# Turning the slots of tokens in SBUF by VectorE, in place, instead of into PSUM by TensorE

## The chip, the cores and the metric

The kernel runs on one core of one Trainium2 chip. The metric is device time in microseconds, here the median of three executions: 631.35 us before the change (630.63 to 631.54).

## The reference

Two layers follow each other. The first is attention with a window of 64 positions (batch 8, 8 heads, 576 positions, head size 64). The second sends each of the 4608 tokens (512 wide) to the one of 8 experts that its gate prefers:

```python
logits = x @ w_gate + modality_bias[modality_id]
e_idx = np.argmax(logits, axis=1)
...
for e in range(E):
    mask = e_idx == e
    h = np.maximum(x[mask] @ w1[e], 0.0)
    out[mask] = gate_w[mask, None] * (h @ w2[e])
```

An expert has w1 of 512 x 1024 and w2 of 1024 x 512. All data are float32.

## The kernel before

**Attention.** The 4608 positions are 72 blocks of 64, and a step handles two of them (a pair, 128 tokens); there are 36 pairs and some steps of run-out. A step s does, in this order on TensorE: the product with the values of pair s-2 (`values`), the gate's logits of pair s-3, the scores of pair s (`scores`), the transposes of the probabilities of pair s-1, the transposes of the finished rows xa of pair s-2 (`x_t`), and two transposes of coming q or k heads (`heads_t`, copied out to qT or kT in `heads_out`). VectorE finds minima, copies qT and kT, divides (`values_out`, which writes xa) and does the routing. GpSimd scatters the finished rows, each with its gate and its token number behind it (514 floats), to `xs_scratch` in HBM, sorted by expert.

**Slots.** A slot is 256 rows of one expert that lie next to each other in `xs_scratch`. `slot_pieces` is a generator that writes the work of slots piece by piece; 16 pieces make a slot. From step 12 on, attention takes one piece at each of four gaps in a step (`gap`), so that a slot spans four steps; when attention is over, the pieces follow each other without attention between them. Two weight buffers hold the weights of two experts. In this execution 8 slots are read while attention runs, and 11 after it, the last of them with 128 rows. TensorE takes float32 data in one pass as fp32r; each product is therefore made of three, with every operand split into a high part (hi, rounded to fp32r) and the rest (lo). Per slot:

- `fetch` and `load_slot` (L250, L203) issue the load of the next slot's rows to xt from SP, ahead of need. xt has one buffer.
- The rows are turned, so that the model dimension lies on partitions. Partition p of piece c holds column 4p + c, to match the rows of w1; so a turn reads every fourth column, 16 bytes from element to element.
- `split` (L194) writes the high part xh (ScalarE, L195) and the low part xl (VectorE, L196) of the turned tokens.
- `first` (L306): 12 matmuls of 256 columns into one PSUM tile, called for k = 0 to 3 and i = 0, 1. After i = 1 comes relu to hh (ScalarE, L326) and the rest hl (VectorE, L327).
- `second` (L330): 6 matmuls of 512 columns from hh and hl into y, for both halves t of the slot, one k later.
- `finish` (L346): y times the gate on VectorE, and an indirect DMA from GpSimd to the output rows.

**Two ways to turn.** A slot that is fetched during attention is loaded by one DMA of 256 rows and turned by TensorE (L281): eight 128x128 transposes against the identity, four into a PSUM bank for each half of the model dimension. A slot that is fetched after attention is loaded by "quarters" (L210): four DMAs that each fill 32 partitions, token w*32 + p going to partition p of a quarter, with 128 columns (512 bytes) in each quarter, and a fifth DMA for gate and number. In this layout the turn needs 32x32 blocks only, and VectorE makes it (L276): four transposes of 128x256 from SBUF into two PSUM banks. Both ways end in PSUM, and the split reads PSUM.

**What sets the order.** The kernel writes the order of the instructions on all engines by hand (`manual_schedule`); each engine runs its own list in order. Work that must not stand in front of a piece's matmuls is put off: functions go to the list `later`, and `run_later` writes them out at fixed places in a step, behind the pieces. Within a slot with k = 3 the pieces are first(3,0), first(3,1), second(2,0), second(2,1), second(3,0), then first(0,0) and first(0,1) of the next slot, and second(3,1). The split's first half is put behind second(2,0), its second half behind second(2,1). The next slot is fetched before first(2,1) during attention and before first(1,0) afterwards. SP issues the loads of v, q, k, weights and slots on one queue, in the order in which the steps write them. The list `last` is empty until the steps of attention are written and non-empty from then on.

Of the kernel before, what the change touches and what calls it, by code (L numbers as in the profile page):

```python
# [8 lines left out]
F32 = mybir.dt.float32  # L9
F32R = mybir.dt.float32r  # L10
BF16 = mybir.dt.bfloat16
I32 = mybir.dt.int32
# [7 lines left out]
P = 128  # L20
# [6 lines left out]
def tile_window_attn_moe(  # L27
# [12 lines left out]
    nc = tc.nc  # L40
    B, H, S, D = q.shape
    N = B * S
    DM = H * D
# [3 lines left out]
    R32 = 32  # L47
    NR = P // R32
# [7 lines left out]
    TP = 2 * P  # L56
# [18 lines left out]
    NC1 = DM // P  # L75
# [53 lines left out]
    def tick(n=1, table=False):  # L129
        for _ in range(n):  # L130
            if routing and not table:
                routing.pop(0)()
            elif queue:
                queue.pop(0)()
                issued[0] += 1
# [58 lines left out]
    def split(ps, hi, lo):  # L194
        nc.scalar.copy(out=hi, in_=ps)  # L195
        nc.vector.tensor_tensor(out=lo, in0=ps, in1=hi.bitcast(F32), op=ALU.subtract)  # L196
# [6 lines left out]
    def load_slot(row_ap, late, nb, quarters):  # L203
        rb = nc.values_load(row_ap, engines=[ET.SP], min_val=0, max_val=DUMMY)
        xt = epool.tile([P, 2, ROW], F32, name="xt")
        rows = xs_blk[bass.ds(rb, nb)]
        if not quarters:
            parts = [(xt[:, 0:nb], rows.rearrange("b p c -> p b c"))]
        else:
            parts = [(x_of(xt)[r * R32:(r + 1) * R32, 0:nb].rearrange("p b w d c -> p b w (d c)"),  # L210
                      rows[:, :, r * P:(r + 1) * P].rearrange("b (w p) c -> p b w c", p=R32)) for r in range(NR)]
            parts.append((tail_of(xt)[:, 0:nb], rows[:, :, DM:ROW].rearrange("b p c -> p b c")))
        for dst, src in parts:
            ins = nc.sync.dma_start(out=dst, in_=src)
            if late is not None:
                tc.declare_no_dep(ins.ins, group=late, reason="rows written before are read")
                tc.add_to_no_dep_group("early_loads", ins.ins)
        return xt

    def x_of(xt):  # L220

        flat = xt.rearrange("p b c -> p (b c)")
        return flat[:, 0:2 * DM].rearrange("p (b w d c) -> p b w d c", b=2, d=R32, c=NC1)
# [5 lines left out]
    last = []  # L229
    position = [-4]  # L230
# [4 lines left out]
    later = []  # L235
    scattered = []

    def bank(i):

        if i == 0 or not last and i == 1:  # L240
            return ps_m.tile([P, 512], F32, name="em")
        if i == 1:
            return ps_s.tile([P, 512], F32, name="sp0")
        return ps_t.tile([P, 512], F32, name="tp")
# [5 lines left out]
    def fetch():  # L250
        if fetched:
            return fetched.pop(0)
        row, late, buf, whichever, need = todo.pop(0)
        assert late is not None or not pads
        assert late is None or late in scattered
        tick(need - issued[0], table=True)
        nb = 1 if whichever == NANY else 2
        quarters = bool(last)
        xt = load_slot(row, late, nb, quarters)
        return dict(xt=xt, buf=buf, any=whichever, nb=nb, quarters=quarters,  # L260
                    tail=tail_of(xt) if quarters else xt[:, :, DM:])

    def slot_pieces():


        def x_turn(sl, i, tp=None):

            xt, nb = sl["xt"], sl["nb"]
            if ("tp", i) in sl or nb == 1 and i == 0:
                return  # L270
            tp = sl["tp", i] = tp or bank(2 if i and (last or not sl["quarters"]) else 0)
            cs_ = range(2 * i, 2 * i + 2) if nb == 2 else range(NC1)
            for n, c in enumerate(cs_):
                cols = slice(n * nb * P, (n + 1) * nb * P)
                if sl["quarters"]:
                    nc.vector.transpose(  # L276
                        out=tp[:, cols].rearrange("p (w t) -> p w t", t=R32),
                        in_=x_of(xt)[:, 0:nb, :, :, c].rearrange("p b w d -> p (b w) d"))
                    continue
                for t in range(nb):  # L280
                    nc.tensor.transpose(  # L281
                        out=tp[:, cols][:, t * P:(t + 1) * P].bitcast(F32R),
                        in_=xt[:, t, c:DM:NC1].bitcast(F32R), identity=ident_r)

        def x_split(sl, i):

            nb = sl["nb"]
            x_turn(sl, i)
            if i == 0:
                sl["x"] = [epool.tile([P, NC1 * TP], F32R, name=nm) for nm in ("xh", "xl")]  # L290
                if nb == 1:
                    return
            hi, lo = (x[:, (2 * i * TP if nb == 2 else 0):][:, 0:512] for x in sl["x"])
            split(sl.pop(("tp", i)), hi, lo)
            if i == 1:
                sl["gate"] = epool.tile([P, 2], F32, name="gate", bufs=2)
                nc.gpsimd.tensor_copy(out=sl["gate"][:, 0:nb], in_=sl["tail"][:, 0:nb, 0])
                sl["id"] = epool.tile([P, 2], I32, name="id", bufs=2)
                nc.gpsimd.tensor_copy(out=sl["id"][:, 0:nb], in_=sl["tail"][:, 0:nb, 1])

        def x_part(sl, i, tp=None):
            if not sl["quarters"]:
                x_turn(sl, i, tp)
            later.append(lambda: x_split(sl, i))

        def first(sl, k, i):  # L306

# [104 lines left out]
        NK = NC2 // 2  # L412

        sl = fetch()
# [8 lines left out]
        while True:  # L423
            nxt = None
            for k in range(1, NK):
                for i in range(2):
                    if (k, i) == ((1, 0) if last else (2, 1)) or k == 2 and i == 1 and nxt is None:
                        assert todo
                        nxt = fetch()
                    first(sl, k, i)  # L430
                    if k == NK - 1 and i == 0 and last and nxt["quarters"]:
                        later.append(lambda: (x_turn(nxt, 0), x_turn(nxt, 1)))
                    yield
                for t in range(2):
                    second(sl, k - 1, t)
                    if k == NK - 1 and nxt and t == 1:
                        x_part(nxt, 1)
                    yield
                    if k == NK - 1 and nxt and t == 0:
                        x_part(nxt, 0)  # L440
                        run_later()
            second(sl, NK - 1, 0)
            yield
            if nxt["nb"] == 1:
                break
            first(nxt, 0, 0)
            yield
            first(nxt, 0, 1)
            yield
            second(sl, NK - 1, 1)  # L450
            yield
            sl = nxt
# [31 lines left out]
    epool = actx.enter_context(tc.tile_pool(name="epool", bufs=1))  # L484
# [402 lines left out]
    def keep_warm(n):  # L887
# [5 lines left out]
    ident_r = const.tile([P, P], F32R, name="ident_r")  # L893
# [5 lines left out]
        out=brow, in_=mod_bias.rearrange("(o m) e -> o m e", o=1).broadcast_to([P, 2, E]))  # L899
# [19 lines left out]
    for h in range(2):  # L919
# [3 lines left out]
        for m in range(3):  # L923
            nc.gpsimd.affine_select(
                out=masks[rows, m, own], in_=masks[rows, m, own],
# [4 lines left out]
            else:  # L930
                nc.gpsimd.affine_select(
                    out=masks[rows, m, before], in_=masks[rows, m, before],
# [5 lines left out]
    for t in xas:  # L938
# [4 lines left out]
        out=tri, in_=tri, compare_op=ALU.is_gt, fill=0.0, base=0,  # L943
# [79 lines left out]
    for s in range(NPR + 4):  # L1023
# [52 lines left out]
        if heads:  # L1076
            tp = turn_bank(s)
# [8 lines left out]
        if R >= 0:  # L1086
            tp = turn_bank(s)
# [10 lines left out]
        if heads:  # L1098
            tp = turn_bank(s)
# [138 lines left out]
    while next(it, "end") != "end":  # L1238
        run_later()
        tick(4)  # L1240
        t = position[0]
# [3 lines left out]
        for n in range(RAWS):  # L1245
            if n < len(swaps) and n == len(ahead) and swaps[n][0] <= t + RAWS:
                _, buf, x, c = swaps[n]
# [18 lines left out]
    with tc.If(trip > 0):  # L1266
        NS = N // P + E
        with ExitStack() as gctx:
# [4 lines left out]
            for st in (1, 2, 4):  # L1273
# [4 lines left out]
            cs_ = gen.tile([1, E], F32, name="cs_")  # L1278
# [22 lines left out]
                out=eoff, in0=desc[0:1, 0, :], scalar1=-1.0, scalar2=float(E), op0=ALU.mult, op1=ALU.add)  # L1301
# [3 lines left out]
                out=gtab[:, :, 1], in0=rw, scalar1=float(E - 1), scalar2=None, op0=ALU.min)  # L1305

            with tc.For_i(0, trip, 1) as it:
# [3 lines left out]
                xt = gen.tile([P, ROW], F32, name="gxt")  # L1311
# [7 lines left out]
                for c in range(NC1):  # L1319
                    wt = gen.tile([P, F], F32, name="gw1", bufs=2)  # L1320
                    nc.sync.dma_start(out=wt, in_=w1_v[bass.ds(ee, 1), :, c, :].rearrange("o p f -> (o p) f"))
                    for n in range(F // 512):
                        nc.tensor.matmul(
                            out=hps[n], lhsT=xT[:, c * P:(c + 1) * P], rhs=wt[:, n * 512:(n + 1) * 512],
# [5 lines left out]
                for n in range(F // 512):  # L1330
                    tp = gps.tile([P, 512], F32, name="gxp")
# [5 lines left out]
                for c2 in range(NC2 // 2):  # L1337
                    wt = gen.tile([P, 2, DM], F32, name="gw2", bufs=2)
                    nc.sync.dma_start(
                        out=wt, in_=w2_v[bass.ds(ee, 1), :, 2 * c2:2 * c2 + 2, :].rearrange("o p c f -> (o p) c f"))  # L1340
                    for i in range(2):
                        c = 2 * c2 + i
                        nc.tensor.matmul(
                            out=yp, lhsT=hT[:, c * P:(c + 1) * P], rhs=wt[:, i, :],
# [3 lines left out]
                    out=y, in0=yp, scalar1=xt[:, DM:DM + 1], scalar2=None, op0=ALU.mult)  # L1348
# [3 lines left out]
                    out=out, out_offset=bass.IndirectOffsetOnAxis(ap=oi, axis=0),  # L1352
                    in_=y, in_offset=None, bounds_check=N - 1, oob_is_err=False)
# [31 lines left out]
```

## Time and profile before

| what | value |
|---|---|
| median of 3 runs | 631.35 us (630.63 to 631.54) |
| the profiled execution's own time | 630.53 us |
| its span, first to last instruction | 628.8 us |
| TensorE (PE) busy | 611.0 us, 97%, 6429 matmuls |
| VectorE (DVE) busy | 383.9 us, 61% |
| ScalarE (ACT) busy | 296.8 us, 47% |
| GpSimd (POOL) busy | 136.1 us, 22% |
| SP's DMA queue | 67.45 MB, 41.6% of the DMA engines' time |

Rows of a timeline read: start in us, length in us, engine, line, operation, out<-in by tile names, shape, count; in brackets the idle time of the engine just before, and what ended it. PE is matmuls and transposes on TensorE, and matmuls are pipelined, so that rows overlap. Names of tiles: xt is a slot's rows, xh and xl the split tokens, hh and hl the split hidden layer, em, tp, sp and y PSUM tiles, xa finished attention rows, Whi and Wlo the split weights.

### The profile page before, as it was taken

The numbers are of one execution on the slowest core, as the hardware profiler recorded it, in microseconds if no ns is written. First come the engines' busy times: TensorE is split into PE (matmuls) and PEld (weight loads), VectorE is DVE, ScalarE is ACT, GpSimd is POOL, SyncE is SP. The second block draws the span as 40 slices with busy tenths as digits, with TensorE's granted clock in tenths as the row PEclk, the third lists the DMA queues.
The fourth block names the chain that finished last, engine by engine and source line by source line (L and its number), as shares of the span: only waits on it lengthen the run. The fifth ranks groups of instructions, "written<-read, shape, count | busy, mean of one in ns | idle before, by whom it ended". The sixth has DMA issues, their size and how long they took to land. (4 is left out here: it accounts for less than half of the span.)

```text
span 628.8 us, 17271 instructions
## 1 busy us (share of the span) xinstructions
PE 611.0 (97%) x6429; PEld 549.2 (87%) x6429; DVE 383.9 (61%) x1493; ACT 296.8 (47%) x933; POOL 136.1 (22%) x315
## 2 busy tenths in 40 slices
PE   8899799999999999999999999999999999999996
PEld 5788688989898899989898899999899999989986
DVE  4899878766676765656655266324434743876721
ACT  4899785656556554645553111111113522564411
POOL 5423412222222320320323130011011011101102
PEclk9999999999999999999999999999999999999999
DMA  9999846675467544452412132732332653578300
GB/s 177 220 240 242 236 123 181 173 200 171 111 163 194 143 120 103 136 152 60 127 53 85 51 102 71 217 118 67 85 118 76 191 165 96 190 244 252 112 11 27
DMA packets 150230, 88.07 MB, mean 140 GB/s; under 512 B 120010, under 2 KB 130816, under 8 KB 150016
## 3 DMA queue, kind: packets, MB, share of 16 engines
q1 hardware_dynamic: 141568, 67.45, 41.6%
q0 software_dynamic: 5888, 18.93, 8.0%
q8 instruction: 51, 0.84, 0.5%
q10 hardware_dynamic: 2688, 0.58, 0.5%
q14 instruction: 35, 0.29, 0.2%
HBM read 67.49 MB, written 23.91 MB: 145 GB/s over the span
## 5 line engine op out<-in xcount | busy, mean ns | idle before, releaser
L340 PE MATMUL y<-Whi,hh 128*128 128x512 f32 x288 | 117.0, 406 | 0.0
L649 ACT ACTIVATE ss<-ss,mn 128x128 f32<-128x128 f32 x288 | 112.6, 398 | 2.0 <-DVE mn L637 2.0
L340 PE MATMUL y<-Wlo,hh 128*128 128x512 f32 x288 | 112.7, 391 | 0.0
L340 PE MATMUL y<-Whi,hl 128*128 128x512 f32 x288 | 112.6, 391 | 0.0
L351 POOL DMA_INDIRECT out_dram<-y,id x36 | 37.4, 1040 | 248.3 <-DVE y L348 165.4
L327 DVE SCALAR_TENSOR_TENSOR hl<-em,hh 128x512 fp32r<-128x512 f32 x50 | 34.5, 690 | 92.3 <-ACT hh L326 89.6
L318 PE MATMUL em<-xh,Whi 128*128 128x256 f32 x400 | 83.7, 291 | 0.0
L326 ACT ACTIVATE hh<-em 128x512 fp32r<-128x512 f32 x50 | 29.6, 593 | 106.1 <-PE em L318 102.1
L318 PE MATMUL em<-xl,Whi 128*128 128x256 f32 x400 | 79.3, 279 | 0.0
L318 PE MATMUL em<-xh,Wlo 128*128 128x256 f32 x400 | 79.2, 279 | 0.0
L637 DVE CUSTOM_DVE_ANT_0 ss<-sp,masks 128x128 f32<-128x128 f32 x288 | 63.6, 286 | 11.9 <-PE sp L623 10.5
L658 ACT COPY pT<-tp 128x512 f32<-128x512 f32 x57 | 31.4, 590 | 74.7 <-PE tp L481 74.0
L340 PEld LDWEIGHTS y<-Whi,hl 128*128 128x128 f32 x288 | 54.1, 188 | 12.2
L318 PEld LDWEIGHTS em<-xh,Whi 128*128 128x128 f32 x400 | 62.3, 189 | 2.0 <-DVE xl L196 0.2
L340 PEld LDWEIGHTS y<-Whi,hh 128*128 128x128 f32 x288 | 54.2, 188 | 8.2
L340 PEld LDWEIGHTS y<-Wlo,hh 128*128 128x128 f32 x288 | 54.2, 188 | 7.8
L318 PEld LDWEIGHTS em<-xl,Whi 128*128 128x128 f32 x400 | 60.9, 188 | 0.0
L318 PEld LDWEIGHTS em<-xh,Wlo 128*128 128x128 f32 x400 | 60.9, 188 | 0.0
L649 ACT ACTIVATION_READ_ACCUMULATOR ss<-ss,mn 128x1 f32 x288 | 56.1, 195 | 0.0
L776 POOL DMA_INDIRECT xs_scratch<-xa,idx x36 | 36.4, 1012 | 82.5 <-DVE lm L719 27.2
L326 ACT ACTIVATE hh<-sp 128x512 fp32r<-128x512 f32 x22 | 13.2, 598 | 76.0 <-PE sp L318 74.0
L675 PEld LDWEIGHTS av<-ve,pT 128*64 128x64 f32 x576 | 36.3, 138 | 12.1 <-issue 5.7
(251 smaller groups left out, 1231.0 us busy)
## 6 DMA issues: line engine op xcount, KB each, us to landing
vo<-in_v_dram SPq DMA_DIRECT2D x32, 256.0 KB
y<-in_moe_w_dram SPq DMA_DIRECT2D x32, 256.0 KB
vo<-in_moe_w_dram SPq DMA_DIRECT2D x24, 256.0 KB
ss<-in_moe_w_dram SPq DMA_DIRECT2D x24, 256.0 KB
xt<-xs_scratch SPq DMA_DIRECT2D x40, 128.0 KB
xt<-xs_scratch SPq DMA_DIRECT2D x8, 514.0 KB
xs_scratch<-xs_scratch SPq DMA_DIRECT2D x8, 514.0 KB
pT<-in_moe_w_dram SPq DMA_DIRECT2D x16, 256.0 KB
```

The lines of the kernel that those rows point to most:

```text
L318: nc.tensor.matmul(out=hb[:, i * TP:(i + 1) * TP], lhsT=w[buf][:, c0:c0 + P], rhs=x[:, c * TP:(c + 1) * TP], start=(n == 0), stop=(n == le ...
L326: nc.scalar.activation(out=hh, in_=hb, func=AF.Relu),
L327: nc.vector.scalar_tensor_tensor(out=hl, in0=hb, scalar=0.0, in1=hh.bitcast(F32), op0=ALU.max, op1=ALU.subtract)))
L340: nc.tensor.matmul(out=sl["y", t], lhsT=h[:, i * TP + t * P:i * TP + (t + 1) * P], rhs=w[buf][:, c0:c0 + DM], start=(k == 0 and n == 0), s ...
L351: ins = nc.gpsimd.indirect_dma_start(out=out, out_offset=bass.IndirectOffsetOnAxis(ap=sl["id"][:, t:t + 1], axis=0), in_=y, in_offset=None ...
L637: nc.vector.tensor_tensor_reduce(out=ss[a][:, hp, :], in0=sp[a][:, hp * P:(hp + 1) * P], in1=mask, scale=-1.0 / 8.0, scalar=3.0e38, op0=AL ...
L649: nc.scalar.activation(out=ss[a][:, hp, :], in_=ss[a][:, hp, :], func=AF.Exp, bias=mn[:, h:h + 1], scale=-1.0, accum_out=sm[:, h:h + 1])
L658: nc.scalar.copy(out=pT, in_=pp)
L675: nc.tensor.matmul(out=av[c * W64:(c + 1) * W64, 2 * hp + a], lhsT=pT[:, i:i + W64], rhs=(vo if c else ve)[p][:, 2 * hp + a, :], start=Tru ...
L776: ins = nc.gpsimd.indirect_dma_start(out=xs, out_offset=bass.IndirectOffsetOnAxis(ap=idx[:, j:j + 1], axis=0), in_=xg[j], in_offset=None)
```

## The change

All slots but the first (those fetched when `position[0] > 0`) are loaded by quarters and turned by VectorE. The turn no longer goes to PSUM: `x_turn` transposes the 32x32 blocks of xt in place, two instructions of 128x512, each over two of the four column groups c. The split reads the turned tokens from xt in SBUF, ScalarE for xh and VectorE for xl, with steps of 16 bytes. The turn is put in `later` behind first(3,0) after attention, as before, and behind first(3,1) during attention; in both cases it comes behind what was put there earlier. Only the first slot is still turned by TensorE.

```diff
-        quarters = bool(last)
+        quarters = bool(position[0] > 0)
...
+        def x_turn(sl):
+
+            blocks = x_of(sl["xt"])[:, 0:sl["nb"]].rearrange("p b w d c -> p (b w) c d")
+            for c in range(0, NC1, 2):
+                nc.vector.transpose(out=blocks[:, :, c:c + 2], in_=blocks[:, :, c:c + 2])
+
+        def x_part(sl, i, tp=None):
...
+            cs_ = slice(2 * i, 2 * i + 2) if nb == 2 else slice(0, NC1)
+            hi, lo = (x[:, cs_.start * nb * P:][:, 0:512] for x in sl["x"])
+            if sl["quarters"]:
+                tp = x_of(xt)[:, 0:nb].rearrange("p b w t c -> p c (b w) t")[:, cs_]
+                hi, lo = (x.rearrange("p (c w t) -> p c w t", w=nb * NR, t=R32) for x in (hi, lo))
+            else:
+                tp = tp or bank(2 if i else 0)
+                for n, (c, t) in enumerate((c, t) for c in range(cs_.start, cs_.stop) for t in range(nb)):
+                    nc.tensor.transpose(
+                        out=tp[:, n * P:(n + 1) * P].bitcast(F32R), in_=xt[:, t, c:DM:NC1].bitcast(F32R),
+                        identity=ident_r)
+
+            def out_():
+                split(tp, hi, lo)
...
+            later.append(out_)
...
-                    if k == NK - 1 and i == 0 and last and nxt["quarters"]:
-                        later.append(lambda: (x_turn(nxt, 0), x_turn(nxt, 1)))
+                    if k == NK - 1 and i == (0 if last else 1) and nxt["quarters"]:
+                        later.append(lambda: x_turn(nxt))
```

More of the change, by code (lines that the diff above doesn't have):

```diff
@@ L263, in slot_pieces @@
     def slot_pieces():
-        def x_turn(sl, i, tp=None):
-            xt, nb = sl["xt"], sl["nb"]
[L269 to L288, printed above, removed]
+        def x_turn(sl):
[3 more added lines that the diff above has]
+        def x_part(sl, i, tp=None):
+            xt, nb = sl["xt"], sl["nb"]
             if i == 0:
@@ L292, in x_split @@
                     return
[L293 to L304, printed above, removed]
+            cs_ = slice(2 * i, 2 * i + 2) if nb == 2 else slice(0, NC1)
[11 more added lines that the diff above has]
+                split(tp, hi, lo)
+                if i == 1:
+                    sl["gate"] = epool.tile([P, 2], F32, name="gate", bufs=2)
+                    nc.gpsimd.tensor_copy(out=sl["gate"][:, 0:nb], in_=sl["tail"][:, 0:nb, 0])
+                    sl["id"] = epool.tile([P, 2], I32, name="id", bufs=2)
+                    nc.gpsimd.tensor_copy(out=sl["id"][:, 0:nb], in_=sl["tail"][:, 0:nb, 1])
+            later.append(out_)
         def first(sl, k, i):
```

## The prediction

> **What bounds the kernel now.** First the busy time by stretch: the attention steps after the first slot (100 to 365 us) and the slots that follow attention (365 to 600). Behind the length come busy us of PE, weight loads, DVE, ACT and POOL, then the granted clock.
>
> ```profile
> 100.00:365.00 265.00, 263.65 (x3255) 237.42 (x3254) 166.14 (x789) 144.38 (x499) 65.51 (x134) 1.00 0.46 127
> 365.00:600.00 235.00, 235.00 (x1534) 214.43 (x1533) 128.56 (x255) 68.85 (x127) 30.78 (x70) 1.00 0.46 141
> ```
>
> TensorE is busy 263.65 of 265 us and then 235.00 of 235, at full clock, while VectorE has 63% and 55%. The table of waits agrees: TensorE's longest wait in the whole execution, five times added up, is this one.
>
> ```profile
> PE av L675 <- POOL ve L547: 3.0, 5, 0.8
> ```
>
> So the time is TensorE's list of instructions, in order. Taking one out shortens the run, unless TensorE then arrives somewhere before its operand. The same stretch for the transposes of line 281 alone shows how many go:
>
> ```profile
> 100.00:365.00 265.00, 9.73 (x56) 9.17 (x56) 1.00 0.46 127
> ```
>
> These 56 are 8 in each of seven slots, four per half. The first slot is turned before 100 us and the change leaves it alone; the slots after 365 us are turned by VectorE already.
>
> **What the removal is worth.** Pipelined matmuls overlap, so their durations (9.73 us in all) are no price; I take starts. The TensorE timeline around the first four of one slot:
>
> ```profile
> 157.72 0.60 PE L481 MATMUL tp<-ident_r,qk 128*128 128x128 f32 x4
> 158.13 0.77 PE L281 MATMUL em<-ident_r,xt 128*128 128x128 f32 x4
> 158.73 0.46 PE L340 MATMUL y<-Whi,hh 128*128 128x512 f32 x1
> ```
>
> around the second four:
>
> ```profile
> 159.96 0.40 PE L340 MATMUL y<-Whi,hl 128*128 128x512 f32 x1
> 160.20 0.63 PE L281 MATMUL tp<-ident_r,xt 128*128 128x128 f32 x4
> 160.75 0.27 PE L675 MATMUL av<-ve,pT 128*64 128x64 f32 x1
> ```
>
> and the same two places in the next step, which has no turn:
>
> ```profile
> 169.32 0.60 PE L481 MATMUL tp<-ident_r,qk 128*128 128x128 f32 x4
> 169.67 0.47 PE L340 MATMUL y<-Whi,hh 128*128 128x512 f32 x1
> ```
> ```profile
> 170.90 0.40 PE L340 MATMUL y<-Whi,hl 128*128 128x512 f32 x1
> 171.23 0.27 PE L675 MATMUL av<-ve,pT 128*64 128x64 f32 x1
> ```
>
> From L481 to L340 it is 1.01 us with the first four and 0.35 without; from the last L340 to L675 0.79 with the second four and 0.33 without. That is 0.66 + 0.46 = 1.12 us a slot, and 7 x 1.12 = 7.84 us. This is the whole gain on offer; the rest of the working asks how much of it is waited away.
>
> **What is added on VectorE.** Each of the seven slots gets two in-place transposes of 128x512, and both halves of its split read SBUF with 16 bytes from element to element. The groups by form give the rates.
>
> ```profile
> L276 DVE STREAM_TRANSPOSE em<-xt 128x256 f32<-128x256 f32 x20 | 12.9, 645 | 1.6 <-DMA xt<-xs_scratch 1.1
> L276 DVE STREAM_TRANSPOSE tp<-xt 128x128 f32<-128x128 f32 x4 | 1.7, 419 | 0.1
> L348 DVE TENSOR_SCALAR y<-y,gate 128x512 f32<-128x512 f32 x36 | 26.9, 748 | 13.7 <-issue 10.5 <-PE y L340 2.8
> L402 DVE TENSOR_SCALAR y<-y,gate 128x256 f32<-128x256 f32 x2 | 1.0, 484 | 3.9 <-PE y L391 3.9
> ```
>
> Transposes that read with the same 16-byte steps cost (645 - 419)/128 = 1.77 ns per element, dense work (748 - 484)/256 = 1.03. At 1.77 a 128x512 transpose takes 0.419 + 384 x 0.00177 = 1.10 us. The subtraction of a split, if its strided operand costs the same difference, grows by 512 x 0.74 ns = 0.38 us. Neighbours on VectorE overlap by 0.08 us (below, 157.38 + 0.69 against 157.99), so the addition is 2 x 1.02 + 2 x 0.38 = 2.80 us a slot. The bounds: at the dense rate a transpose takes 0.419 + 384 x 0.00103 = 0.81 us and the splits grow by nothing; if the strided write, which no row here shows, is paid for behind the read, the transposes' 2.04 us double. I take the middle: the 1.77 was measured on this very operand, and an engine that pipelines reading and writing pays the slower of the two once. On ScalarE the copies to xh may grow likewise; it is busy 144.38 us of 265 and hides that.
>
> [...]
>
> **Where it stands and who waits.** The turn comes behind hl of the last half on VectorE's queue. Behind the turn stand the rank (L757), the copy of qT (L588, for which scores wait), routing, a piece of Wlo, both xl, and xa (L683), for which the transposes of xa on TensorE wait; last the minima. The VectorE timeline of the slot above, from hl on:
>
> ```profile
> 157.38 0.69 DVE L327 SCALAR_TENSOR_TENSOR hl<-em,hh 128x512 fp32r<-128x512 f32 x1 [0.30 <-ACT hh L326]
> 157.99 0.17 DVE L757 TENSOR_TENSOR tgt<-tp,ebase 128x16 f32<-128x16 f32 x1
> 158.36 0.69 DVE L588 COPY qT<-tp 128x512 f32<-128x512 f32 x1 [0.20 <-PE tp L481]
> ```
>
> its second xl, its xa, and the TensorE row that wants xa:
>
> ```profile
> 161.48 0.69 DVE L196 TENSOR_TENSOR xl<-tp,xh 128x512 fp32r<-128x512 f32 x1 [0.70 <-ACT xh L195]
> ```
> ```profile
> 162.37 0.69 DVE L683 TENSOR_TENSOR xa<-av,rs 128x512 f32<-128x512 f32 x1
> ```
> ```profile
> 165.62 0.60 PE L481 MATMUL tp<-ident_r,xa 128*128 128x128 f32 x4
> ```
>
> Between hl and xa VectorE idles 0.20 + 0.70 = 0.90 us; that cover goes first. xa then ends at 162.37 + 0.69 - 0.90 + 2.80 = 164.96, and TensorE wants it at 165.62 - 1.12 = 164.50: a new wait of 0.46 us. The slot at 202 us has the same list, so 0.46 again. The slot at 114 has less idle to fill:
>
> ```profile
> 117.83 0.69 DVE L196 TENSOR_TENSOR xl<-tp,xh 128x512 fp32r<-128x512 f32 x1 [0.39 <-ACT xh L195]
> ```
> ```profile
> 118.72 0.69 DVE L683 TENSOR_TENSOR xa<-av,rs 128x512 f32<-128x512 f32 x1
> ```
> ```profile
> 121.95 0.60 PE L481 MATMUL tp<-ident_r,xa 128*128 128x128 f32 x4
> ```
>
> xa ends at 118.72 + 0.69 - 0.39 + 2.80 = 121.82, wanted at 120.83: 0.99 us. Later slots have more. The sixth:
>
> ```profile
> 332.90 0.69 DVE L196 TENSOR_TENSOR xl<-em,xh 128x512 fp32r<-128x512 f32 x1 [0.79 <-ACT xh L195]
> 334.83 0.69 DVE L196 TENSOR_TENSOR xl<-tp,xh 128x512 fp32r<-128x512 f32 x1 [1.23 <-ACT xh L195]
> ```
> ```profile
> 335.72 0.69 DVE L683 TENSOR_TENSOR xa<-av,rs 128x512 f32<-128x512 f32 x1
> ```
> ```profile
> 338.49 0.60 PE L481 MATMUL tp<-ident_r,xa 128*128 128x128 f32 x4
> ```
>
> 335.72 + 0.69 - 2.02 + 2.80 = 337.19, wanted at 337.37: no wait, 0.18 us to spare. The fourth and fifth get the same. The seventh, at the end of attention, has no xa, but its xl is wanted at once:
>
> ```profile
> 363.22 0.69 DVE L196 TENSOR_TENSOR xl<-em,xh 128x512 fp32r<-128x512 f32 x1 [0.79 <-ACT xh L195]
> 365.16 0.69 DVE L196 TENSOR_TENSOR xl<-tp,xh 128x512 fp32r<-128x512 f32 x1 [1.24 <-ACT xh L195]
> ```
> ```profile
> 366.96 0.40 PE L318 MATMUL em<-xl,Whi 128*128 128x256 f32 x2
> ```
>
> 365.16 + 0.69 - 2.03 + 2.80 = 366.62 against 366.96 - 1.12 = 365.84: 0.78 us. The waits together: 0.99 + 2 x 0.46 + 0.78 = 2.69 us.
>
> **Parts costed at nothing.** Loads: one DMA becomes five. In the late slots SP issues five in 2.48 us, and VectorE was released 4.6 us after the first issue:
>
> ```profile
> 398.49 2.48 SPq L214 DMA_DIRECT2D xt<-xs_scratch  x5
> ```
> ```profile
> 403.14 1.32 DVE L276 STREAM_TRANSPOSE em<-xt 128x256 f32<-128x256 f32 x2 [1.11 <-DMA xt<-xs_scratch]
> ```
>
> The slot above is issued here:
>
> ```profile
> 149.22 0.38 SPq L214 DMA_DIRECT2D xt<-xs_scratch  x1
> ```
>
> It is turned from 157.99 on, 8.8 us later, so the data have 4 us to spare; without that cover VectorE and all behind it would wait for what is missing. Queued behind on SP are pieces of weights, v, q and k, each 2 us later and wanted about a step later (11.6 us, 157.72 to 169.32).
>
> The slots after 365 us lose no TensorE work. Their four transposes become two, some 0.4 us shorter by the same rate, and their xl 0.76 us longer: the second xl of the fullest slot ends at 586.94 + 0.67 - 0.4 + 0.76 = 587.97, wanted at 588.83.
>
> ```profile
> 586.94 0.67 DVE L196 TENSOR_TENSOR xl<-tp,xh 128x512 fp32r<-128x512 f32 x1
> ```
> ```profile
> 588.83 0.40 PE L318 MATMUL em<-xl,Whi 128*128 128x256 f32 x2
> ```
>
> Also xt is held until its split has read it, so SP issues the next load, and the weights queued behind it, a few us later; a late slot (144 matmuls in the code, of 1534 in 235 us) takes 22 us, which hides it.
>
> **Sum.** -7.84 + 2.69 = -5.15 us. The profiled execution took 630.53 (span 628.8), so 625.4; it lies 0.8 below the median of 631.35, so a median of 626.2 us.
>
> **Rivals.** A, the cover holds nearly everywhere: the splits read at the dense rate, the addition is 2.04 us, and only the slots at 114 (0.23 us) and 365 (0.02) wait. Gain 7.6: 623.8 us. For it: TensorE has slack in every other step; against it: the 1.77.
>
> B, slower: the in-place transposes pay on the write as well. With x us more per slot the waits are 2.69 + 4x + 3(x - 0.18), and they eat the 7.84 us at x = 0.81, when one transpose takes 1.51 us where I say 1.10. Doubled (x = 2.04) they are 16.4 us: 631.35 + 8.6 = 639.9 us. For it: seven turns stand in a queue with under 1 us to spare. Against it: the copy of qT (L588) writes SBUF in steps of two elements and takes the 0.69 us of a dense write. [...]
>
> C, no change: something else behind the turn (the minima, hence the exponentials) is late by as much as TensorE gains. 631.3 us. Against it: ScalarE's load, above.
>
> **How the numbers follow.** Forecast 0.50 (its own range 624.9 to 628), A 0.26, B 0.15, C 0.09. The range starts a little under A, 623.2, and goes up to C, 631.0, leaving out most of B. Faster by over 0.2% (1.3 us, about what a measurement of this kernel can tell): 0.77; within: 0.09; slower: 0.14.
>
> **What would show it.** L281 keeps 8 transposes, all before 100 us. The turn has 128x512 forms at about 1.10 us; at 1.51 or more B is right. The subtraction to xl takes 1.06 us (forecast) or 0.69 (A). TensorE gets new waits at L481 for xa in the slots near 114, 158 and 202. If TensorE stays without a wait and the gain is still well under 7 us, my 1.12 us a slot is wrong; if VectorE waits for xt, the loads are.

## The result, and the profile after

The changed kernel is slower. The median of five runs is 635.26 us (634.46 to 636.64) against 630.86 us for the kernel before beside it: a ratio of 1.0069, with a 95% interval of 1.0055 to 1.0084. The prediction was 626.2 us. The profiled execution has a span of 633.5 us against 628.8.

The diff shifts line numbers. The lines that matter below, before and then after: the turn 276 and 270, transposes of xa, qk and the probabilities 481 and 475, the copy of qT 588 and 582, the copy of the probabilities 658 and 652, values 675 and 669, xa 683 and 677, logits 700 and 694, their addition 705 and 699.

The same two stretches as in the prediction, in the busy time by stretch of the changed kernel (us of PE, weight loads, DVE, ACT, POOL, then the granted clock):

```profile
100.00:365.00 265.00, 254.21 (x3187) 226.67 (x3186) 180.03 (x799) 150.15 (x501) 65.43 (x134) 1.00 0.48 128
365.00:600.00 235.00, 234.69 (x1524) 213.43 (x1523) 137.75 (x246) 81.81 (x129) 30.54 (x67) 1.00 0.45 140
```

After attention almost nothing has changed (234.69 of 235 busy). During attention TensorE idles 265 - 254.21 = 10.8 us, where it idled 1.35. The clock is full in both (1.00), so this is waiting. The table of TensorE's waits names it; first the kernel before:

```profile
PE tp L481 <- DVE lg L705: 2.1, 3, 1.2
PE tp L481 <- DVE xa L683: 1.5, 1, 1.5
...
PE tp L481 <- ACT pT L658: 1.0, 1, 1.0
```

and the changed kernel (total us, times, longest):

```profile
PE tp L475 <- DVE lg L699: 8.8, 6, 2.5
PE tp L475 <- ACT pT L652: 3.0, 3, 1.3
...
PE tp L475 <- DVE xa L677: 2.4, 2, 1.5
```

The new waits, 8.7 us more in the first two rows, are at transposes that wait for `lg`, the addition of the bias to the gate's logits on VectorE, and for `pT`, ScalarE's copy of transposed probabilities. For xa, where the prediction put them, there is 0.9 us more, in one place at 351 us, where the prediction had none. The groups by form show that the work itself cost what was forecast (mean ns of one is the number behind the comma):

```profile
L270 DVE STREAM_TRANSPOSE xt<-xt 128x512 f32<-128x512 f32 x34 | 36.1, 1110 | 1.4 <-DMA xt<-xs_scratch 1.3
L196 DVE TENSOR_TENSOR xl<-xt,xh 128x512 fp32r<-128x512 f32 x35 | 36.4, 1075 | 2.6 <-ACT xh L195 2.5
L195 ACT CAST xh<-xt 128x512 fp32r<-128x512 f32 x35 | 37.6, 1125 | 4.2 <-DVE xt L270 3.9
```

Now the slot whose timeline the prediction used. VectorE of the changed kernel:

```profile
159.73 2.15 DVE L270 STREAM_TRANSPOSE xt<-xt 128x512 f32<-128x512 f32 x2
161.79 0.12 DVE L751 TENSOR_TENSOR tgt<-tp,ebase 128x16 f32<-128x16 f32 x1
161.84 0.67 DVE L582 COPY qT<-tp 128x512 f32<-128x512 f32 x1
...
163.55 2.06 DVE L196 TENSOR_TENSOR xl<-xt,xh 128x512 fp32r<-128x512 f32 x2
165.81 0.69 DVE L677 TENSOR_TENSOR xa<-av,rs 128x512 f32<-128x512 f32 x1
166.42 0.15 DVE L699 TENSOR_TENSOR lg<-tp,bias_sel 128x8 f32<-128x8 f32 x1
```

and TensorE at the same time:

```profile
162.36 0.59 PE L694 MATMUL tp<-wg,xaT 128*64 128x8 f32 x16
...
163.92 0.66 PE L475 MATMUL tp<-ident_r,ss 128*128 128x128 f32 x4
...
166.72 0.63 PE L475 MATMUL tp<-ident_r,ss 128*128 128x128 f32 x4 [2.15 <-DVE lg L699]
```

A step writes the logits, then the first four transposes of the probabilities, then the other four, each into a PSUM tile `tp`, and there are two such tiles (`ps_t` has bufs=2). The other four therefore need the tile of the logits, and that comes free when VectorE has read it: at 166.57, behind the turn, qT, both xl and xa. In the kernel before, the same chain was early enough:

```profile
162.98 0.16 DVE L705 TENSOR_TENSOR lg<-tp,bias_sel 128x8 f32<-128x8 f32 x1
```
```profile
163.29 1.09 PE L481 MATMUL tp<-ident_r,ss 128*128 128x128 f32 x8
```

All eight transposes ran in one go there, the fifth at about 163.29 + 0.55 = 163.84 (half of 1.09), and lg had ended at 163.14. So 0.7 us were to spare, and VectorE was made 1.9 us later (2.80 less 0.90 of idle) while TensorE came 1.12 earlier.

**Where the time went, step by step.** Comparing the starts of the values in the two traces, the execution after is 1.2 us later at 65 us and still at 105 us, ahead of any slot that the change touches. Five variants below, with the same instructions on TensorE up to there, are 0.2 to 1.4 us earlier than the kernel before at 105 us, so this is not the change's, and I leave it out. The seven steps that lost a turn are shorter by 1.12, 1.12, 1.10, 1.04, 1.04, 1.45 and 1.33 us, 8.2 in all (7.84 forecast). The following stretches are longer by 1.69, 2.32, 2.73, 1.39, 1.34, 1.43 and 0.86, 11.8 in all (2.69 forecast). Net 3.6. What ends TensorE's wait in these stretches is lg in the slots at 158, 202, 246 and 290 us (7.8 of the 11.8), pT in those at 114 and 332, xa at 351, and xl at the end of attention. Where it is pT, the other four transposes start ahead of lg (at 114: 121.63 against 123.03), so the logits' tile is not what holds them there. From 370 us to the end the distance between the traces stays at 4.7 us.

### The profile page after: what moved, and what is told of

The parts are those of the page before. It is cut to its first block, busy times and chain, and to the rows that moved or that the text cites. A ratio compares the mean times of both kernels' runs of the same rounds, so it can differ in the third digit from the quotient of the medians.

```text
span 633.5 us, 17288 instructions
## 1 busy us (share of the span) xinstructions
PE 607.3 (96%) x6373; PEld 543.1 (86%) x6373; DVE 406.6 (64%) x1485; ACT 315.2 (50%) x933; POOL 136.1 (21%) x315
```

## The experiments

All times are beside runs of the kernel before (medians of 630.5 to 631.5 us), and ratios are to that kernel. Gains over the changed kernel are differences of medians; by the ratios, those of 12.0, 8.3, 8.3 and 9.1 us below are 11.7, 7.4, 7.6 and 8.9.

**The late slots alone.** The changed kernel, with only the slots after attention turned in place:

```diff
-        quarters = bool(position[0] > 0)
+        quarters = bool(last)
```

> Only the slots after attention are turned in place; the slots read during attention are loaded and turned by TensorE as before. Theory (all of the change's loss arises in attention, because the four late steps compared in the two traces keep one offset of 4.73 us from 370 us to the end): 630.9 us, no change from before. Rival (the longer splits and the longer hold on xt in the late slots cost time too): 632 us or more.

Measured 630.69 us, 1.0002 (0.9991 to 1.0013). The late part costs and gains nothing; all of the loss is made in attention.

**The logits' tile freed by another engine.** In the changed kernel ScalarE copies the logits out of PSUM, and VectorE adds the bias from SBUF:

```diff
+        raw = small.tile([P, E], F32, name="raw")
+        nc.scalar.copy(out=raw, in_=lt[:, 0:E])
         nc.vector.tensor_tensor(
-            out=st[G, "lg"][:, j, :], in0=lt[:, 0:E], in1=bias_sel[:, p, :], op=ALU.add)
+            out=st[G, "lg"][:, j, :], in0=raw, in1=bias_sel[:, p, :], op=ALU.add)
```

> The changed kernel, but ScalarE copies the gate's logits out of PSUM into SBUF right behind their matmuls, and VectorE adds the bias from there, so that the PSUM bank no longer waits for VectorE's queue. Theory (the loss is the second half of the probabilities' transposes waiting for the bank that lg on VectorE frees late): that wait goes, about 8 us of the profile; what stays are the waits for xa, 0.5 to 1 us in the first three slots: 626 to 629 us. Rival (VectorE's 2.8 us more push minima and exponentials, and the next wait takes the place of this one): 633 us or more.

Measured 623.25 us, 0.9884 (0.9867 to 0.9900): 12.0 us under the changed kernel, and more than expected. VectorE has as much to do as without the edit (406.7 us busy against 406.6). What TensorE still waits for there:

```profile
PE tp L475 <- DVE xa L677: 1.7, 2, 1.4
...
PE tp L475 <- ACT raw L700: 1.1, 1, 1.1
...
PE tp L475 <- DVE lg L701: 0.9, 3, 0.3
```

The 8.8 us for lg have become 0.9, and these are not for the logits' tile, which lg no longer reads. They are at the transposes of xa, and xa stands just ahead of lg on VectorE:

```profile
164.59 0.69 DVE L677 TENSOR_TENSOR xa<-av,rs 128x512 f32<-128x512 f32 x1
165.20 0.16 DVE L701 TENSOR_TENSOR lg<-raw,bias_sel 128x8 f32<-128x8 f32 x1
```
```profile
165.43 0.63 PE L475 MATMUL tp<-ident_r,xa 128*128 128x128 f32 x4 [0.27 <-DVE lg L701]
```

These are the waits that the prediction had priced: in this run the slot at 158 us loses 0.45 us, that at 202 us 0.50, and those at 246 and 290 us nothing (0.46, 0.46, 0 and 0 forecast). The row for pT is gone from the list, but its 1.28 us at 114 us go on as the 1.1 us for raw, which stands behind the same late weights and the same xh on ScalarE's queue.

**The same edit on the kernel before.** The control, without which the last result would be read as 12 us given back:

> Control: the kernel before with the one edit of the logits (ScalarE copies them out of PSUM, VectorE adds the bias from SBUF). In the profile of before, TensorE waits 2.1 us in all for lg, in three places. Theory (the edit is worth much only where the turn stands in front of lg): 628 to 630 us, a gain of 1 to 2 us. Rival (the edit is a gain of its own that has nothing to do with the turn): 625 us or less.

Measured 627.62 us, 0.9945 (0.9932 to 0.9958): 3.2 us gained, about the sum of the two rows of the kernel before (2.1 and 1.0). So by this control some 3.2 of the 12.0 us have nothing to do with the change. With the tile freed in time on both sides, the change takes 627.62 to 623.25: a gain of 4.4 us (3.9 by the ratios), where the prediction had 5.15.

**The turn earlier in VectorE's queue.** The changed kernel, with the turn behind first(3,0) in attention too:

```diff
-                    if k == NK - 1 and i == (0 if last else 1) and nxt["quarters"]:
+                    if k == NK - 1 and i == 0 and nxt["quarters"]:
```

> The changed kernel with the turn put behind first(3,0) in attention too, one gap earlier, where VectorE idles 1.76 us ahead of the copy of qT. Theory (the place of the turn on VectorE's queue decides, lg comes late by what is not hidden): lg comes 1.7 us earlier in five slots, their waits of 1.3 to 2.7 us fall by about that: 627 to 629 us. Rival (the amount of VectorE work decides, not its place): within 1.3 us of the changed kernel, 635.3. Second rival (the five DMAs land too late for an earlier turn): VectorE waits for xt, and the time is above 635.3.

Measured 626.94 us, 0.9952 (0.9934 to 0.9970), as expected. The waits for lg fall from 8.8 to 3.7 us, and a wait of 1.4 for qT comes up; VectorE also begins to wait for the slot's rows (3.4 us in three places, 1.3 in one before the edit).

**No turn.** For the slots read in attention the turn is left out, so what is computed from those slots is not the reference's:

```diff
-                        later.append(lambda: x_turn(nxt))
+                        if last:
+                            later.append(lambda: x_turn(nxt))
```

> The changed kernel without the two transposes in the slots read during attention (their tokens stay unturned, so the products of those slots mix columns); loads by quarters and strided splits stay. Theory: 2.06 us less ahead of lg per slot, the waits of the first five slots (1.5, 2.3, 2.7, 1.4, 1.3 us) fall to 0, 0.3, 0.7, 0, 0, and the seventh's of 0.9 to 0: 635.3 - 9.1 = 626 us. Rival (loads by quarters or the strided splits cost the time): 632 us or more.

Measured 626.92 us, 0.9948 (0.9931 to 0.9966). So the turns, 2.15 us a slot on an engine that is busy 64% of the time, carry 8.3 us. Waits for lg of 3.9 us are left, where the kernel before has 2.1; the splits still read with 16-byte steps.

**Dense columns.** The columns of xt are read as (c, d) instead of (d, c), so that a turn and both splits read consecutive elements. The rows of w1 keep their order, so the product mixes columns and is not the reference's.

```diff
-        return flat[:, 0:2 * DM].rearrange("p (b w d c) -> p b w d c", b=2, d=R32, c=NC1)
+        return flat[:, 0:2 * DM].rearrange("p (b w c d) -> p b w d c", b=2, d=R32, c=NC1)
```

> The changed kernel with the columns of xt taken as (c, d) instead of (d, c), so that turn and splits run over neighbouring elements instead of 16-byte steps; the rows of w1 aren't reordered to match, so the products of the turned slots mix columns. Same instructions, same loads. Theory (the 16-byte step is what makes a turn take 1.11 us and a subtraction 1.075): 0.81 and 0.69 us, ScalarE's copy 0.6 instead of 1.125; 1.37 us less ahead of lg in each slot, five waits and the seventh slot's shrink by about that: 635.3 - 7 = 628 us. Rival (the transpose is that slow by itself, only the splits get shorter): the turn stays at 1.11 us, 0.77 us less per slot, 631 us.

Measured 626.17 us, 0.9928 (0.9916 to 0.9940). Its groups by form:

```profile
L273 DVE STREAM_TRANSPOSE xt<-xt 128x512 f32<-128x512 f32 x34 | 22.0, 687 | 0.1
L196 DVE TENSOR_TENSOR xl<-xt,xh 128x512 fp32r<-128x512 f32 x35 | 22.5, 682 | 0.9 <-ACT xh L195 0.9
L195 ACT CAST xh<-xt 128x512 fp32r<-128x512 f32 x35 | 20.2, 619 | 2.3 <-DVE xt L273 2.3
```

Against 1110, 1075 and 1125 ns this is 2 x 0.423 + 2 x 0.393 = 1.63 us a slot less on VectorE; 9.1 us are gained, 1.3 us a slot. In the slots at 158 and 202 us, where some wait is left, the step is 1.6 us shorter than in the changed kernel: there a microsecond on VectorE is a microsecond of time. In those at 246 and 290 us the whole 1.4 and 1.3 us are gone.

**The load later.** The next slot's load is issued one piece later, so that SP's five issues come behind more of the weights; alone, and with the logits by ScalarE:

```diff
-                    if (k, i) == ((1, 0) if last else (2, 1)) or k == 2 and i == 1 and nxt is None:
+                    if (k, i) == ((1, 0) if last else (3, 0)) or k == 3 and i == 0 and nxt is None:
```

> The changed kernel, with the next slot fetched one gap later during attention (before first(3,0) instead of first(2,1)), so that the five issues of a slot's load stand behind a piece of weights on SP's queue, not ahead of it. lg stays on VectorE. Theory (in the first turned slot ScalarE waits 1.9 us for a piece of weights that SP issued 3 us later than before, and xh, pT and TensorE behind it): the 1.5 us of that slot fall to about 1 (lg's wait is next there), the other slots stay: 634.3 to 635.3 us. Rival (loads are then too late for the turn): VectorE waits for xt, 637 us or more.

> The same later fetch together with ScalarE's copy of the logits. Without lg in the way, the weights' lateness is what is left of the first turned slot's 1.5 us. Theory: 1 to 1.5 us under the 623.25 us of the kernel with that copy alone, 621.8 to 622.3 us. Rival (late loads): 624 us or more.

Measured 636.43 us, 1.0094 (1.0081 to 1.0107), and 629.33 us, 0.9979 (0.9969 to 0.9988): the theory missed both times, and the second run, 6.1 us slower than the same kernel with the load in its place, is the rival's. VectorE now waits for the rows themselves; its table of waits, first of the run with both:

```profile
DVE xt L270 <- DMA xt<-xs_scratch: 6.0, 4, 1.8
```

and in the changed kernel:

```profile
DVE xt L270 <- DMA xt<-xs_scratch: 1.3, 1, 1.3
```

The load had little to spare where it stood, and everything behind the turn stands behind this wait too.

**The logits ahead of the values.** The changed kernel, with `logits(s - 3)` and the routing that follows it written ahead of `values(s - 2)` and `values_out(s - 2)`, so that lg no longer stands behind xa:

> The changed kernel, with one thing moved: the logits and their addition on VectorE stand ahead of the values and of xa's division, where they stood behind both. The addition then ends about 0.6 us earlier against the two xl (it no longer stands behind the 0.69 us of xa), and xa 0.15 us later. If what TensorE waits for is the bank that the logits hold, the five waits of the trace (8.8 us) become shorter by 0.6 us each, 3.0 us in all: 632.3 us. Rival, xa is what the steps wait for (as the prediction had it): nothing gained, up to 0.15 us lost a step, 635.3 to 636.5 us. Rival, the order on TensorE decides (the logits before the values make the values late): above 636 us.

Measured 633.69 us, 1.0040 (1.0024 to 1.0056). By the ratios 1.8 us are gained, in the direction of the theory, and less than the 3.0 expected. The waits for lg are gone from the head of the list, and this took part of the gain:

```profile
PE tp L694 <- ACT xaT L686: 3.4, 4, 1.8
PE y L694 <- ACT xaT L686: 2.1, 3, 0.9
```

The logits, now earlier, wait for their own operand.

**Both cures.** The turn one piece earlier, as in the run above, and the logits by ScalarE:

> The changed kernel with the logits copied out by ScalarE and also the turn queued two pieces earlier in attention. Alone the two gave 12.0 and 8.3 us. Both act on the same wait, so they do not add up: what is left with the logits by ScalarE alone is 1.7 us of waits for xa, 0.9 for the logits and 1.1 for the copy. If VectorE's queue is the cause of all of these, they fall by half or more: 621.5 to 622.3 us. Rival: the earlier turn makes qT late instead (a wait of 1.4 us in the run with the turn early), and nothing is gained: 623 to 624 us.

Measured 624.72 us, 0.9888 (0.9870 to 0.9906), the same as with the logits by ScalarE alone: the rival was right that nothing is gained. In this trace VectorE waits 4.7 us for the slot's rows, and TensorE 1.6 us for qT.

**Dense, with the weights in the same order.** To both cures are added dense columns, w1's rows loaded to match, and the first slot by quarters too:

```diff
-            nc.sync.dma_start(
-                out=raw, in_=w1_v[bass.ds(ev, 1), :, ch, f0:f0 + WCH].rearrange("o p f -> (o p) f"))
+            for r in range(NR):
+                nc.sync.dma_start(
+                    out=raw[r * R32:(r + 1) * R32],
+                    in_=w1_v[bass.ds(ev, 1), r, ch, :, f0:f0 + WCH].rearrange("o d f -> (o d) f"))
```

> The same as the run with both (logits by ScalarE, turn early), and in addition columns of xt as (c, d): the splits read rows of consecutive elements, and the rows of w1 are loaded in the same order, by four transfers a piece instead of one, so the product is the reference's; the first slot is loaded by quarters and turned by VectorE too. Turn 0.69, xl 0.68 and xh 0.62 us are expected (as with mixed columns), 1.6 us less on VectorE in a slot. If VectorE's queue is what costs, the last waits go: 620.5 to 621.5 us. Rival: SP becomes late, since each piece of w1 now takes four issues (about 0.5 us each by the rows of the five issues of a slot, 2.49 us), and the weights come late: 624 us or more. The first slot's turn on VectorE can cost up to 2 us at the start.

Measured 633.32 us (628.71 to 637.73), 1.0030 (1.0004 to 1.0055): the rival. Transposes and splits take 688 and 683 ns, but the weights come late, in ScalarE's table of waits:

```profile
ACT Whi L116 <- DMA vo<-in_moe_w_dram: 14.9, 8, 3.9
...
ACT Whi L116 <- DMA ss<-in_moe_w_dram: 5.3, 7, 1.4
```

Most of these waits cost no time. Beside the trace of the run with both cures, this one is 3.0 us later at 92 us, behind the first slot's turn, and 4.1 us later at 561. By 583 us it is 10.5 us later, and that is made by one piece of weights, in whose wake hh comes late on ScalarE and the matmuls on TensorE:

```profile
583.58 0.62 ACT L116 CAST Whi<-vo 128x512 fp32r<-128x512 f32 x1 [3.91 <-DMA vo<-in_moe_w_dram]
...
585.05 0.59 ACT L324 ACTIVATE hh<-sp 128x512 fp32r<-128x512 f32 x1
```
```profile
585.70 0.79 PE L338 MATMUL y<-Whi,hh 128*128 128x512 f32 x1 [2.81 <-ACT hh L324]
```

With the 2.81 us of waiting comes a lower granted clock, 0.52 in the next stretch, where it is 1.00 in the 83 us ahead:

```profile
585.00:592.00 7.00, 5.86 (x19) 4.75 (x20) 6.12 (x11) 4.05 (x8) 0.74 (x1) 0.52 0.56 145
```

**The second slot left as it was.** In the run with the logits by ScalarE, the slot read at about 114 us goes by TensorE again:

```diff
-        quarters = bool(position[0] > 0)
+        quarters = bool(position[0] > 20)
```

> The changed kernel with the logits by ScalarE; the first slot that the change turns on VectorE (read at about 114 us) is loaded in one transfer and transposed by TensorE as before, the other slots as in the changed kernel. In that slot the run with the logits by ScalarE gained 1.12 us of transposes and lost 1.50 us one step later, where a piece of weights came late behind the five issues on SP. If the five issues are the cause of that, leaving them out gains 0.3 to 0.5 us: 622.8 us. Rival: the piece is late for another reason (the step loses its 1.5 us anyway), then the slot loses the 1.12 us of its transposes: 624.4 us.

Measured 626.26 us, 0.9918 (0.9901 to 0.9934), by the ratios some 2 us slower than with that slot changed, so by the time the rival's side. The traces do not place this loss in the slot. From the values ahead of it to those two steps on (105 to 128 us) it is 22.55 us with the slot changed, 22.17 here and 22.17 in the kernel before: 1.12 us of transposes come back, 1.50 us of waiting go, and 0.38 us are gained, as the theory had it. ScalarE's wait for the piece of weights is 2.1 us with the slot changed and 0.8 here. Why the median is 2 us longer all the same is open. Of the difference between the two traces, 0.6 us lie ahead of the slot, and the steps that end near 182 and 225 us are 0.3 and 0.4 us longer. Nor does this run separate the five issues from the longer splits, since both go with the slot's turn.

## Why the prediction was wrong

**The gain: right.** 56 transposes went (6429 matmuls became 6373), and the steps without them are shorter by 1.04 to 1.45 us; 1.12 was forecast. The first slot alone keeps its eight.

**The addition on VectorE: right.** The prediction had 1.10 us for a transpose and 1.06 for a subtraction; 1.110 and 1.075 were measured. So rival A (dense rates) and rival B (the write pays too, 1.51 us or more) are out as mechanisms: B's side came, by another way. The read in steps costs time: the subtraction, of which only a read has 16-byte steps, takes 1075 ns against 682 dense. A write in such steps beside the read adds nothing here, as the prediction assumed in taking the middle: a 128x256 transpose takes 645 ns where it reads in steps and writes PSUM, and 631 in place.

**Who waits: the step that failed.** The prediction named "xa (L683), for which the transposes of xa on TensorE wait", and priced the waits at 2.69 us. The row behind xa on VectorE, lg, has a consumer that comes 1.8 us sooner than xa's (163.84 against 165.62 in the slot at 158 us): the second half of the probabilities' transposes, which needs not lg but the PSUM tile that lg reads from. No row shows a tile as the price of its reuse, so following results from row to row did not find it; yet a wait of that kind stood in the table of before, three times, 2.1 us. Had it been used, the prediction's own numbers would have given the size: for the slot at 158 us lg ends at 163.14 + 1.90 = 165.04 and is wanted at 163.84 - 1.12 = 162.72, a wait of 2.3 us (2.15 measured). In the slot at 202 us:

```profile
206.65 0.16 DVE L705 TENSOR_TENSOR lg<-tp,bias_sel 128x8 f32<-128x8 f32 x1
```
```profile
206.96 1.09 PE L481 MATMUL tp<-ident_r,ss 128*128 128x128 f32 x8
```

lg ends at 206.81, is made 2.80 - 0.85 later by the same rule (its idle there is 0.17 + 0.68), and is wanted at 206.96 + 0.55 - 1.12: 2.4 us, and 2.52 were measured. With xa itself the prediction was right as far as it went: once the tile is freed by ScalarE, the losses that it priced come out as 0.45 and 0.50 us.

**The parts costed at nothing.** The late slots cost nothing, as said. The five issues did not: "weights, v, q and k, each 2 us later and wanted about a step later" fails at the slot at 114. ScalarE's queue of the changed kernel there:

```profile
118.41 0.62 ACT L114 CAST Whi<-y 128x512 fp32r<-128x512 f32 x1 [1.86 <-DMA y<-in_moe_w_dram]
...
118.94 2.17 ACT L195 CAST xh<-xt 128x512 fp32r<-128x512 f32 x2
```

The piece is late by 1.86 us, xh, xl and pT stand behind it, and TensorE waits 1.28 us for pT there. The splits on ScalarE, held to be hidden by its load of 144 us in 265, add 1.08 us in the same place: a mean share was used where a queue was meant. With dense columns, where the splits on ScalarE are short and the piece is late by 2.4 us, the step still loses 1.04 us, against 1.52 in the changed kernel; so about 1 us of it goes with the late weights.

**Rival C** said that something else behind the turn would be late. It did not name lg, and its price, as much as TensorE gains, was too low. The slot at the end of attention was priced well: 0.78 us forecast, 0.86 found.

**What is shown and what is not.** That the tile of the logits carries the loss is shown by freeing it elsewhere (12.0 us, of which 3.2 with the control), and by the three ways of shortening what stands ahead of it (8.3, 8.3 and 9.1 us). For the slot at 114 us, that its loss comes with the slot's change is shown by the run that leaves it as it was (22.17 us as before); that about 1 us of it is the late weights rests on the traces alone. The version to keep is the changed kernel with the logits copied out by ScalarE: 623.25 us, 1.2% under the kernel before.

## What to carry to other kernels

When work is put into an engine's queue, go through every instruction behind it and ask two questions: who reads its result, and who needs the buffer that it reads from. The second waiter was the earlier one here, by 1.8 us in the slot at 158 us, and with a ring of two PSUM tiles an instruction of 0.15 us held TensorE for 2.15 us there. An engine that had little to do in the mean (63% before, 68% after) was still the last at one place of a step, six times (8.8 us of waits for lg), and moving that one short read of 0.15 us to another queue turned a loss of 4.4 us into a gain.

## What the runs showed of the hardware

In the trace of before, the matmuls of `first`, with fp32r operands, have one row of TensorE each (1728 at L318 for 12 in each of 8 calls in 18 slots), and those of the logits, with float32 operands, two (576 at L700 for the 8 that the code writes in each of 36 pairs). The size of the loss by stride on ScalarE had not been forecast: its copy of 128x512 takes 1125 ns with 16-byte steps and 619 dense, 506 ns more, where VectorE's subtraction takes 393 more (1075 against 682). A strided write beside a strided read added nothing to a transpose on VectorE (631 ns in place, 645 into PSUM). The run with w1's pieces of 256 KB loaded as four transfers of 64 KB, dense columns and the first slot turned on VectorE was 8.6 us slower than without these three (633.32 against 624.72). Its trace is 10.4 us longer than that run's (631.7 against 621.3): 3.0 us of it are there behind the first slot, and 6.4 come with one late piece of weights, which left TensorE idle for 2.81 us and was followed by a granted clock of 0.52 in the 7 us from 585 on.
